# Linear attention and a mixture layer on one core: the denominators' signs summed in PSUM, their products moved to the end of the next pair's visit, and a new order

## The chip, the cores and the metric

The kernel runs on one core of a Trainium2 chip. The time is the device time of one execution in microseconds (us). Five queues work side by side on the core: TensorE (PE in the profile, PEld for its weight loads), VectorE (DVE), ScalarE (ACT), GpSimd (POOL) and SyncE (SP, which here only issues DMAs). Each of them takes its instructions strictly in the order in which the program has them, and an instruction that has to wait holds up all that stand behind it in its queue.

## The reference

There are 8 batches, 8 heads, 576 positions and a head dimension of 64. The features of queries and keys, `phi`, have 2 x 128 columns: the exponentials of both signs of a projection from which its largest absolute value has been taken. The output of the attention, with heads side by side, goes into a layer with 1024 hidden columns.

```
def phi(x):
    proj = einsum('bhsd,df->bhsf', x, w_phi)
    proj = proj - max(abs(proj), axis=-1, keepdims=True)
    return concatenate([exp(proj), exp(-proj)], axis=-1)
kv  = einsum('bhsf,bhsd->bhfd', phi(k), v)
z   = sum(phi(k), axis=2)
num = einsum('bhsf,bhfd->bhsd', phi(q), kv)
den = einsum('bhsf,bhf->bhs', phi(q), z) + 1e-06
x   = (num / den), heads joined: 4608 x 512
h   = x @ w_in
e   = exp(h - max(h));  solu = h * e / (sum(e) + 1e-09)
ln  = (solu - mean(solu)) / sqrt(var(solu) + 1e-06) * g_ln
out = ln @ w_out
```

So each position of each head has one denominator, a sum over 256 features, of which one half belongs to the sign + and one half to the sign -.

## The kernel before

**Tiling.** Two heads make a pair: there are 32 pairs. Two pairs make a unit `u`, of which there are 16, two for each batch; `sub` is the pair within the unit and `n = 2u + sub` its number. In a pair `j` is the head, `s` the sign and `c` the half of the 576 positions, 288 (`HC`) at a time. The second layer works on 36 tiles of 128 positions ("MoE" in names and comments). Nine of these tiles need the two batches of four units, and the last five of all need the last pair.

**What a pair does.** Keys are projected (`pjk`), reduced to their largest absolute value (`m`), subtracted (`dk`) and exponentiated (`ek`). A *visit* of TensorE (`visit`) then multiplies them with the values into the bank `kvT`, and at its end multiplies the summed exponentials `zacc` with ones (`kv_z`), so that `z` comes out 32 times over. VectorE turns the bank (`kvs`) and two steps of DMAs (`dk` in DRAM, then `kvf`) put it where it serves as weights. The queries are loaded by two DMAs of the same data, one for each half of the partitions (`rawq`), rounded (`hq`), corrected on GpSimd, projected (`pq`), turned (`blk`), given their maximum (`mtp`, `mt`, `mb`, `mcp`, `mcol`), turned back (`pT`) and exponentiated (`fq`).

**Numerators and denominators.** `q_num` multiplies `fq` with `kvf` into two banks `num`, one for each half of the positions. From pair 5 to pair 30 this stands at the *beginning* of the visit of the next pair (`JOIN = 6`); for the other six it is an operation of its own. `q_den` is always an operation of its own. It fills two banks `den`, one for each half of the positions; in each of them the rows 32 x (2s + j) and the 31 behind hold sign `s` of head `j`, 32 times the same row. ScalarE copies all four banks (`E`, `dE`). Then follows a chain over DRAM: `den_rows` stores each 32nd row of `dE` (`d<-dE`); `den_load` brings the 4 x 576 numbers back as 128 partitions x 2 signs x 9 (`cmp<-d`); VectorE adds the signs and the small constant and takes the reciprocal of 9 columns (`cmp`, `cmr`); `den_store` stores it (`d<-cmr`); `den_bcast` loads it in two DMAs to 64 partitions each (`rb<-d`). GpSimd multiplies `E` by `rb` (`divide`) into `xa` or `xb`, which the second layer reads.

**The second layer.** For each tile: `mxh` and `mxl` (two roundings of the input), `h` (24 matmuls in two halves), the maximum `nm`, the exponential `eu`, the product, the variance, the transpose `uT` in two parts, `uh` and `ul`, `o` (24 matmuls in two halves), `os` and the store of the output. These tiles are what TensorE does between the steps of the attention.

**What sets the order.** All operations are written down with an engine, a charged duration, their predecessors and the buffers that they take (`Plan.op`). `Plan.order` plays the program through, one operation at a time, with these durations. Where several operations are ready on an engine it takes the one with the smallest priority. The priority is the sum of two numbers from tables, `BASE` (the weights, the 16 units, the 36 tiles) and `OFFSET` (each kind of operation). A change of TensorE's tiled mode is charged (`SWITCH`) and avoided (`STICK`, `LINGER`). The result is one sequence, in which the instructions are emitted; on the chip each queue keeps its part of that sequence and waits by semaphores for what it needs. The charges and priorities have no other effect on the chip.

**Buffers.** There are three PSUM banks of the kind `a`. `pjk`, `pq`, `mtp`, `mcp`, `num` and `den` share them. There is one bank for `kvT`, and there are two tiles each for `E`, `dE` and `kvf` and one for `rb`.

The instructions go through a helper that keeps them in program order. For this reason nearly all rows of the profile name the same line, L347, and are told apart by the names of what they write and read.

Of the kernel before, what the change touches and what calls it, by code (L numbers as in the profile page):

```python
# [44 lines left out]
    rk=4, rv=5, xh=2, xl=2, m=3, d=3, e=6, za=2, kf=2, q4=5, m4=2, mt=2, mb=2, E=2, dE=2, rb=1,  # L45
# [22 lines left out]
)  # L68
OFFSET = (
# [49 lines left out]
)  # L119


# [1182 lines left out]
```

## Time and profile before

| | |
|---|---|
| median of 3 runs | 790.88 us (789.54 to 791.89) |
| the profiled execution, its own time | 790.95 us |
| its span, from the first to the last instruction | 789.2 us |
| granted TensorE clock, mean | 0.994 |
| DMAs issued for the denominators | 32 x (1 + 1 + 1 + 2) |

In a list of stretches, each row has the start and the end, the length, and for each engine its busy time and number of instructions, then the granted clock, the mean busy share of the DMA engines and the GB/s. In a timeline a row has its start, its length, the engine, the operation, what is written and what is read; in brackets stands the time that the engine had been idle, and what ended the idle time. Merged rows carry a count (x16). Rows of one matmul overlap, because matmuls are pipelined: what a matmul costs is read from start to start. In the chain of waits each row is a start, a length and a piece of work that the next one waited for. In a list of waits a row has who waited, for whom, the total in us, how often, and the longest. In a list of groups the last number before the bar is the mean of one instruction in ns, and behind the bar stands the idle time ahead of the group.

### The profile page before, as it was taken

The numbers are of one execution on the slowest core, as the hardware profiler recorded it, in microseconds if no ns is written. First come the engines' busy times: TensorE is split into PE (matmuls) and PEld (weight loads), VectorE is DVE, ScalarE is ACT, GpSimd is POOL, SyncE is SP. The second block draws the span as 40 slices with busy tenths as digits, with TensorE's granted clock in tenths as the row PEclk, the third lists the DMA queues.
The fourth block names the chain that finished last, engine by engine and source line by source line (L and its number), as shares of the span: only waits on it lengthen the run. The fifth ranks groups of instructions, "written<-read, shape, count | busy, mean of one in ns | idle before, by whom it ended". The sixth has DMA issues, their size and how long they took to land.

```text
span 789.2 us, 13661 instructions
## 1 busy us (share of the span) xinstructions
PE 756.7 (96%) x4935; PEld 562.2 (71%) x4935; DVE 486.4 (62%) x829; ACT 405.8 (51%) x814; POOL 470.9 (60%) x507
## 2 busy tenths in 40 slices
PE   5899898999999999999999999999999999999997
PEld 3565586767677777767776777777777776788886
DVE  4978684756675675756566686665756683444343
ACT  3876764564645565454745465463644655322322
POOL 1224897778687678585676759675776855231210
PEclk8999999999999999999999999999999999999999
DMA  6954442443526153442435343333334212200000
GB/s 203 374 122 122 104 103 52 108 110 104 119 73 135 53 123 104 106 100 70 125 81 121 85 108 100 90 88 92 87 99 114 78 43 78 52 28 14 27 28 27
DMA packets 105251, 75.96 MB, mean 96 GB/s; under 512 B 65376, under 2 KB 91488, under 8 KB 104672
## 3 DMA queue, kind: packets, MB, share of 16 engines
q1 hardware_dynamic: 105184, 75.10, 35.9%
q8 instruction: 39, 0.64, 0.4%
q14 instruction: 28, 0.23, 0.1%
HBM read 59.67 MB, written 15.38 MB: 95 GB/s over the span
## 4 chain that ended last, share of the span: by engine, by line
PE 72%; DMA 10%; DVE 5%; ACT 3%; POOL 3%; issue 3%; SPq 3%; ACTq 0%; POOLq 0%; DVEq 0%
PE o L347 21%; PE h L347 20%; PE kvT L347 9%; PE num L347 6%; PE pjk L347 5%; PE uT L347 3%; PE pq L347 3%; DMA rawq<-in_q 3%; PE den L347 3%; SPq L347 3%; DMA cmp<-d 2%; POOL hq L347 2%; DMA dk<-kvs 1%; PE pjq L347 1%; DMA rawk<-in_k 1%
## 5 line engine op out<-in xcount | busy, mean ns | idle before, releaser
L347 PE MATMUL o<-w_out_h,uh 128*128 128x512 f32 x288 | 116.0, 403 | 0.4 <-ACT uh L347 0.4
L347 ACT ACTIVATE ek<-dk 128x512 f32<-128x512 f32 (+1 forms) x160 | 87.2, 584 | 53.6 <-DVE dk L347 49.7
L347 PE MATMUL o<-w_out_h,ul 128*128 128x512 f32 x288 | 114.2, 397 | 0.0
L347 PE MATMUL o<-w_out_l,uh 128*128 128x512 f32 x288 | 113.9, 396 | 0.0
L347 POOL TENSOR_TENSOR zacc<-zacc,ek 128x512 f32<-128x512 f32 (+1 forms) x78 | 100.7, 1290 | 12.8 <-ACT ek L347 8.1
L347 POOL TENSOR_TENSOR hq<-rawq,hq 64x1152 fp32r<-64x1152 f32 x26 | 69.5, 2674 | 47.7 <-ACT hq L347 43.9
L347 PE MATMUL h<-win_h,mxh 128*128 128x512 f32 x288 | 93.6, 406 | 1.0 <-DVE eu L347 1.0
L347 PE MATMUL h<-win_h,mxl 128*128 128x512 f32 x288 | 90.8, 396 | 0.0
L347 PE MATMUL h<-win_l,mxh 128*128 128x512 f32 x288 | 90.6, 396 | 0.0
L347 DVE TENSOR_TENSOR ul<-uT,uh 128x512 fp32r<-128x512 f32 x72 | 48.2, 679 | 54.0 <-ACT uh L347 54.0
L347 ACT ACTIVATE fq<-pT 128x576 f32<-128x576 f32 x104 | 68.6, 688 | 17.3 <-DVE pT L347 14.0
L347 ACT CAST uh<-uT 128x512 fp32r<-128x512 f32 x72 | 41.6, 590 | 61.9 <-PE uT L347 48.8
L347 PE MATMUL num<-fq,kvf 128*64 128x288 f32 x512 | 69.2, 412 | 2.8 <-ACT win_h L347 1.8
L347 ACT ACTIVATE eu<-h,nm 128x1024 f32<-128x1024 f32 x36 | 40.3, 1118 | 57.6 <-DVE nm L347 57.5
L347 DVE TENSOR_REDUCE nm<-h 128x1 f32<-128x1024 f32 x36 | 43.8, 1218 | 41.7 <-PE h L347 41.6
L347 POOL TENSOR_TENSOR blk<-blk,mcol 128x1152 f32<-128x1152 f32 x26 | 55.6, 2137 | 17.2 <-ACT mcol L347 17.1
L347 PE MATMUL kvT<-ek,rawv 128*64 128x256 f32 x512 | 65.3, 387 | 0.0
L347 DVE STREAM_TRANSPOSE blk<-pq 128x288 f32<-128x288 f32 x104 | 46.5, 460 | 28.4 <-PE pq L347 22.8
L347 DVE TENSOR_TENSOR eu<-h,eu 128x1024 f32<-128x1024 f32 x36 | 43.9, 1220 | 32.4 <-ACT eu L347 32.4
L347 PEld LDWEIGHTS o<-w_out_h,ul 128*128 128x128 f32 x288 | 54.2, 188 | 13.6 <-DVE ul L347 0.4
L347 PEld LDWEIGHTS h<-win_h,mxl 128*128 128x128 f32 x288 | 54.2, 189 | 13.1 <-POOL mxl L347 0.2
L347 PEld LDWEIGHTS h<-win_l,mxh 128*128 128x128 f32 x288 | 54.1, 188 | 13.1
(107 smaller groups left out, 1584.1 us busy)
## 6 DMA issues: line engine op xcount, KB each, us to landing
rawq<-in_q SPq DMA_DIRECT2D x52, 288.0 KB
rb<-d SPq DMA_DIRECT2D x64, 144.0 KB
out<-os SPq DMA_DIRECT2D x36, 256.0 KB
rawk<-in_k SPq DMA_DIRECT2D x64, 128.0 KB
rawv<-in_v SPq DMA_DIRECT2D x64, 128.0 KB
dk<-kvs SPq DMA_DIRECT2D x28, 192.0 KB
kvf<-dk SPq DMA_DIRECT2D x112, 48.0 KB
wraw<-in_w_in SPq DMA_DIRECT2D x4, 1024.0 KB
```

The source lines that it names most:

```text
L347: return self.tc.keep_in_program_order(method(*args, **kwargs))
```

## The change

1. **Signs summed in PSUM.** `q_den` fills one bank instead of two. The rows 32 x (2c + j) now belong to half `c` of the positions and head `j`, and the matmul of the sign - is added to that of the sign +. The number and the shapes of the matmuls are as before: eight, each 32 columns of weights and 288 positions.
2. **The products' place.** For pairs 5 to 30 `q_den` stands at the end of the next pair's visit, behind `kv_z`. For the others it remains an operation of its own.
3. **One evacuation, and the reciprocal on VectorE at once.** ScalarE copies 128 x 288 once, and adds the small constant. VectorE inverts these 128 x 288 numbers in place.
4. **A shorter chain of DMAs.** `den_rows` stores each 32nd row of the inverted tile (4 x 288), and two DMAs broadcast it from there, each in two runs of 288 positions. `den_load` and `den_store` are gone. There are two `rb` tiles.
5. **One load of queries.** The input of the queries is laid out with its rows twice, and one DMA of 128 partitions replaces two of 64.
6. **New order.** Both tables are replaced, and several charged durations with them; the charge of the visit has the products in it, and the visit takes all three `a` banks in the plan. In the tables the entry of the weights goes from -200.2 to -223.1 and that of the first unit from -1092.1 to -1390.3.

```
-    ... E=2, dE=2, rb=1,
+    ... E=2, dE=2, rb=2,
...
 def visit(st, sub, before):
...
         kv_z(st, sub)
+    if before:
+        q_den(*before)
...
-def q_load(st, sub, i):
-    if i == 0:
-        st["rq", sub] = sb("q4", [P, 2, S], name="rawq")
-    nc.sync.dma_start(out=st["rq", sub][i * D : (i + 1) * D], in_=qT[st["b"], 2 * st["qd"] + sub])
+def q_load(st, sub):
+    st["rq", sub] = sb("q4", [P, 2, S], name="rawq")
+    nc.sync.dma_start(out=st["rq", sub], in_=qT[st["b"], 2 * st["qd"] + sub])
...
 def q_den(st, sub):
-    for c in range(2):
-        po = st["den", sub, c] = bank("a", [P, 512], "den")
-        for s in range(2):
+    po = st["den", sub] = bank("a", [P, 512], "den")
+    for s in range(2):
+        for c in range(2):
             for j in range(2):
-                r = slice(32 * (2 * s + j), 32 * (2 * s + j) + 32)
+                r, z = 32 * (2 * c + j), 32 * (2 * s + j)
                 nc.tensor.matmul(
-                    po[r, :HC], lhsT=st["kvf", sub][:, 2, r], rhs=st["qf", sub, c][:, j, s],
-                    start=True, stop=True,
+                    po[r : r + 32, :HC], lhsT=st["kvf", sub][:, 2, z : z + 32], rhs=st["qf", sub, c][:, j, s],
+                    start=(s == 0), stop=(s == 1), skip_group_check=True,
                 )
...
+def den_eps(st, sub):
+    st["dens", sub] = sb("dE", [P, HC], name="dE")
+    nc.scalar.activation(out=st["dens", sub], in_=st["den", sub][:, :HC], func=AF.Copy, bias=EPS)
+
+def den_recip(st, sub):
+    nc.vector.reciprocal(out=st["dens", sub], in_=st["dens", sub])
+
 def den_rows(st, sub):
-    st["d1", sub] = dram.tile([4, S], F32, tag="d1", name="d1")
+    st["d1", sub] = dram.tile([4, HC], F32, tag="d1", name="d1")
     nc.sync.dma_start(out=st["d1", sub], in_=st["dens", sub][::32, :])
-
-def den_load(st, sub):
-    st["cmp", sub] = work.tile([P, 2, 9], F32, tag="cmp", bufs=8, name="cmp")
-    nc.sync.dma_start(out=st["cmp", sub], in_=st["d1", sub].rearrange("(s h) (a b) -> (h a) s b", s=2, b=9))
-
-def den_recip(st, sub):
-    c = st["cmp", sub]
-    nc.vector.scalar_tensor_tensor(
-        out=c[:, 0], in0=c[:, 0], scalar=EPS, in1=c[:, 1], op0=ALU.add, op1=ALU.add
-    )
-    st["cmr", sub] = work.tile([P, 9], F32, tag="cmr", bufs=8, name="cmr")
-    nc.vector.reciprocal(out=st["cmr", sub], in_=c[:, 0])
-
-def den_store(st, sub):
-    st["d2", sub] = dram.tile([2, S], F32, tag="d2", name="d2")
-    nc.sync.dma_start(out=st["d2", sub].rearrange("h (a b) -> (h a) b", b=9), in_=st["cmr", sub])
 
 def den_bcast(st, sub, j):
     if j == 0:
         st["rb", sub] = sb("rb", [P, S])
+    src = st["d1", sub].rearrange("(c j) t -> j c t", j=2)[j : j + 1]
     nc.sync.dma_start(
-        out=st["rb", sub][j * D : (j + 1) * D, :], in_=st["d2", sub][j : j + 1, :].to_broadcast([D, S])
+        out=st["rb", sub][j * D : (j + 1) * D, :].rearrange("p (c t) -> p c t", c=2),
+        in_=src.to_broadcast([D, 2, HC]),
     )
...
-add(("qd", sub), "tensor", 2 * mm32(HC), z + 5.5, q_den, (sub,), feat + [source["num"]],
-    [("a", ("den", sub, c)) for c in range(2)], fk, {(u, "qv", sub, 0, "den"): mm32(HC)})
+if not joined:
+    add(("qd", sub), "tensor", 2 * mm32(HC), z + 5.5, q_den, (sub,), feat + [source["num"]],
+        [("a", ("den", sub))], fk)
...
+add(("dc", sub), "vector", dve(HC) + 30, z + 6.3, den_recip, (sub,), [("de", sub)], (), [("dE", sub)])
...
-BASE = (-200.2, -1092.1, ...)
+BASE = (-223.1, -1390.3, ...)
-OFFSET = (...)
+OFFSET = (...)
```

More of the change, by code (lines that the diff above doesn't have):

```diff
@@ L142, in dma @@
 def dma(nbytes, spread=False):
[L143 removed]
+    return (580 if spread else 400), max(nbytes / 360.0, 50)
 class Plan:
@@ L542, in linear_attention_then_moe @@
         op(("wl", i), "sync", dma(8 * P * DF), z - 9, w_load, (i, raw_tag[i] if i < 4 else None), alloc=[(raw_tag[i], R)] if i < 4 else [])
-        op(("ws", i), "scalar", 947, z, w_rebias, (i,), [("wl", i)], tiles=R4)
+        op(("ws", i), "scalar", 1055, z, w_rebias, (i,), [("wl", i)], tiles=R4)
         op(("wb", i, 0), "vector", 600, z, w_bits, (i, 0, w_tag[i]), [("ws", i)], [(w_tag[i], T)], R4)
@@ L550, in linear_attention_then_moe @@
         else:
-            op(("wg", i), "scalar", 1226, z, w_gain, (i,), [("wb", i, 2), "gain"], tiles=[T])
+            op(("wg", i), "scalar", 1260, z, w_gain, (i,), [("wb", i, 2), "gain"], tiles=[T])
     for i in range(5, 8):
@@ L884, in q_den, with q_oe @@
                     )
-    def q_oe(st, sub, c, key):
+    def q_oe(st, sub, c):
         if c == 0:
-            st[key + "s", sub] = sb("E" if key == "num" else "dE", [P, S], name="E" if key == "num" else "dE")
-        nc.scalar.copy(out=st[key + "s", sub][:, c * HC : (c + 1) * HC], in_=st[key, sub, c][:, :HC])
+            st["nums", sub] = sb("E", [P, S], name="E")
+        nc.scalar.copy(out=st["nums", sub][:, c * HC : (c + 1) * HC], in_=st["num", sub, c][:, :HC])
+    def den_eps(st, sub):
+        st["dens", sub] = sb("dE", [P, HC], name="dE")
+        nc.scalar.activation(out=st["dens", sub], in_=st["den", sub][:, :HC], func=AF.Copy, bias=EPS)
@@ L1008, in linear_attention_then_moe @@
                 tiles += [("abs", (pu, "f", ps_, c)) for c in range(2)] + [("abs", (pu, "kf", ps_))]
-                alloc += [("a", ("abs", (pu, "num", ps_, c))) for c in range(2)]
-                early = {(pu, "qv", ps_, c, "num"): cost + (1 - c) * 2 * mm32(HC) for c in range(2)}
-                cost += 4 * mm32(HC)
+                alloc += [("a", ("abs", (pu, "num", ps_, c))) for c in range(2)] + [("a", ("abs", (pu, "den", ps_)))]
+                den = 2 * mm32(HC)
+                early = {(pu, "qv", ps_, c): den + cost + (1 - c) * 2 * mm32(HC) for c in range(2)}
+                early[u, "kve", sub] = den
+                cost += 4 * mm32(HC) + den
             add(("V", sub), "tensor", cost, z, visit, (sub, (states[pu], ps_) if joined else None), after, alloc, tiles,
@@ L1041, in linear_attention_then_moe @@
             if qsp:
-                for i in range(2):
-                    add(("ql", sub, i), "sync", dma(D * 2 * S * 4, True), z - 4, q_load, (sub, i),
-                        [("ql", sub, 0)] if i else (), () if i else [("q4", ("rq", sub))], [("rq", sub)])
-                add(("qh", sub), "scalar", act(2 * S), z - 2.5, q_hi, (sub,), [("ql", sub, 1)], [("q4", ("hq", sub))],
+                add(("ql", sub), "sync", (400, 1640), z - 4, q_load, (sub,), (), [("q4", ("rq", sub))])
+                add(("qh", sub), "scalar", act(2 * S), z - 2.5, q_hi, (sub,), [("ql", sub)], [("q4", ("hq", sub))],
                     [("rq", sub)])
-                add(("qlo", sub), "gpsimd", pool(2 * S), z - 2.2, q_lo, (sub,), [("qh", sub)], (),
+                add(("qlo", sub), "gpsimd", pool(2 * S) + 130, z - 2.2, q_lo, (sub,), [("qh", sub)], (),
                     [("rq", sub), ("hq", sub)])
@@ L1094, in linear_attention_then_moe @@
             joined = JOIN <= n + 1 < 4 * B
-            source = {"num": ("abs", ((n + 1) // 2, "V", (n + 1) % 2)) if joined else ("qo", sub), "den": ("qd", sub)}
+            visitor = ("abs", ((n + 1) // 2, "V", (n + 1) % 2))
+            source = {"num": visitor if joined else ("qo", sub), "den": visitor if joined else ("qd", sub)}
             if not joined:
@@ L1102, in linear_attention_then_moe @@
             for c in range(2):
-                for k, t in (("num", "E"), ("den", "dE")):
-                    add(("qv", sub, c, k), "scalar", act(HC, True), z + 5.1 + c, q_oe, (sub, c, k),
-                        [source[k]] + ([("qv", sub, 0, k)] if c else []),
-                        () if c else [(t, (t, sub))], [(k, sub, c), (t, sub)])
-            add(("dr", sub), "sync", dma(16 * S), z + 6.4, den_rows, (sub,),
-                [("qv", sub, 0, "den"), ("qv", sub, 1, "den")], (), [("dE", sub)])
@@ L1109, in linear_attention_then_moe @@
-            add(("dl", sub), "sync", dma(0), z + 6.8, den_load, (sub,), [("dr", sub)], ())
-            add(("dc", sub), "vector", 330, z + 7.3, den_recip, (sub,), [("dl", sub)])
-            add(("ds", sub), "sync", dma(0), z + 7.4, den_store, (sub,), [("dc", sub)])
+                add(("qv", sub, c), "scalar", act(HC, True), z + 5.1 + c, q_oe, (sub, c),
+                    [source["num"]] + ([("qv", sub, 0)] if c else []), () if c else [("E", ("E", sub))],
+                    [("num", sub, c), ("E", sub)])
@@ L1112, in linear_attention_then_moe @@
+            add(("de", sub), "scalar", act(HC, True), z + 6.0, den_eps, (sub,), [source["den"]], [("dE", ("dE", sub))],
+                [("den", sub)])
+            add(("dc", sub), "vector", dve(HC) + 30, z + 6.3, den_recip, (sub,), [("de", sub)], (), [("dE", sub)])
+            add(("ds", sub), "sync", (330, 100), z + 6.5, den_rows, (sub,), [("dc", sub)], (), [("dE", sub)])
             for j in range(2):
[L1113 to L1114 removed]
+                add(("db", sub, j), "sync", (560, 600), z + 6.9, den_bcast, (sub, j),
+                    [("ds", sub)] + ([("db", sub, 0)] if j else [("db", 0, 1)] if sub else []), () if j else [("rb", ("rb", sub))],
@@ L1115, in linear_attention_then_moe @@
                     [("rb", sub)])
             pair = 2 * qd + sub
-            after = [(u, "db", sub, 1), (u, "qv", sub, 1, "num")] + ([(2 * b, "dv", 0)] if pair else [])
+            after = [(u, "db", sub, 1), (u, "qv", sub, 1)] + ([(2 * b, "dv", 0)] if pair else [])
             op((u, "dv", sub), "gpsimd", pool(S) + (130 if b % 2 else 30), z0 + (z + 8.5) * step, divide,
@@ L1219, in linear_attention_then_moe @@
     op("tail", "gpsimd", 0, 2 * B * UNIT + 40, start_tail, (),
-       [(2 * B - 1, "qv", s, c, k) for s in range(2) for c in range(2) for k in ("num", "den")])
+       [(2 * B - 1, "qv", s, 1) for s in range(2)] + [(2 * B - 1, "de", s) for s in range(2)])
     for t in range(NTOK // P):
@@ L1253, in linear_attention_then_moe @@
             op(n("o", hf), "tensor", 12 * mm(512), z + 13 + 3 * hf, moe_o, (t, hf),
-               [n("ul", hf)] + ([n("o", 0)] if hf else [("wol", f) for f in range(8)] if t == 0 else []),
+               [n("ul", hf)] + ([n("o", 0)] if hf else [("wol", f) for f in range(8)]),
                () if hf else [("mo", n("o"))], [n("uh"), n("ul"), n("o")])
```

22 lines of the change are left out of this document (10 added, 12 removed), and 104 rows, old and new, of tables (BASE, OFFSET).

## The prediction

> **What bounds the kernel now.** I read the page first (busy shares), then the stretches, then the rows of TensorE that follow an idle time, then the chain of waits ahead of those rows. The page:
>
> ```profile
> span 789.2 us, 13661 instructions
> PE 756.7 (96%) x4935; PEld 562.2 (71%) x4935; DVE 486.4 (62%) x829; ACT 405.8 (51%) x814; POOL 470.9 (60%) x507
> ```
>
> TensorE is the bound: it stands idle for 789.2 - 756.7 = 32.5 us in all. The stretches show where:
>
> ```profile
> core 0: us, PE busy (x) PEld busy (x) DVE busy (x) ACT busy (x) POOL busy (x), PEclk, DMA share, GB/s
> 0.00:20.00 20.00, 11.09 (x29) 7.97 (x31) 8.33 (x16) 6.27 (x12) 2.26 (x17) 0.86 0.68 206
> 20.00:40.00 20.00, 17.34 (x141) 11.09 (x143) 18.04 (x24) 17.96 (x33) 4.74 (x2) 0.93 0.99 369
> 340.00:380.00 40.00, 38.26 (x232) 29.63 (x226) 25.20 (x45) 19.67 (x42) 25.06 (x30) 1.00 0.37 95
> ...
> 700.00:740.00 40.00, 40.00 (x185) 32.51 (x184) 16.77 (x22) 9.91 (x17) 7.24 (x15) 1.00 0.06 21
> ```
>
> The first 40 us hold 11.57 us of the idle time, with the DMA engines nearly full in the second half of it. In the middle it comes in pieces (1.74 us in the 40 us from 340). The end (700 to 740) is TensorE without a gap. So a cheaper instruction on another engine gives nothing by itself. Time comes from fewer cycles on TensorE or from an idle time that goes away. The idle times that this change can reach are these:
>
> ```profile
> 36.87 0.55 PE L347 MATMUL dT<-ident,dq 128*128 128x128 f32 x3 [1.61 <-ACT dE L347]
> 70.47 1.13 PE L347 MATMUL pjq<-wph,rawq 128*128 128x256 f32 x4 [0.47 <-DVE dk L347]
> 172.17 0.38 PE L347 MATMUL pjk<-wph_h,xh 128*128 128x256 f32 x1 [1.64 <-ACT dE L347]
> 208.90 0.40 PE L347 MATMUL pq<-hq,w_hh 128*128 128x288 f32 x1 [0.54 <-POOL hq L347]
> 350.62 0.38 PE L347 MATMUL pq<-hq,w_hh 128*128 128x288 f32 x1 [1.33 <-DVE dk L347]
> 432.12 0.69 PE L347 MATMUL den<-fq,kvf 128*32 128x288 f32 x8 [0.51 <-ACT E L347]
> 584.98 0.29 PE L347 MATMUL mtp<-ident,m 128*36 128x128 f32 x1 [1.42 <-DVE m L347]
> ```
>
> Three of them look like VectorE's ordinary work, but the chain of waits ahead of 350.62, and likewise of 432.12, shows what held VectorE:
>
> ```profile
> 347.20 1.89 DMA cmp<-d
> 349.11 0.57 DVE cmp L347
> 349.84 0.64 DVE dk L347
> ...
> 420.90 5.10 DMA cmp<-d
> 426.02 1.57 DVE cmp L347
> 427.83 1.09 DVE nm L347
> ```
>
> VectorE's queue is in order. It stands at the denominators' addition until a DMA has landed, and all that is behind it is late: the keys' subtraction dk at 349.84, the row maximum nm at 427.83. Ahead of 70.47 and 584.98 the chain has the same links.
>
> **The change, part by part.** *The products move (A).* Eight matmuls (16 instructions) before, eight of the same shape after; what can change is the entry to and the exit from the column-tiled mode. The timeline has both places already:
>
> ```profile
> 449.55 0.42 PE L347 MATMUL kvT<-zacc,ones 128*32 128x128 f32 x8
> 449.91 0.41 PE L347 MATMUL pq<-hq,w_hh 128*128 128x288 f32 x1
> ...
> 463.73 0.40 PE L347 MATMUL o<-w_out_l,uh 128*128 128x512 f32 x1
> 463.96 0.39 PE L347 MATMUL o<-w_out_h,ul 128*128 128x512 f32 x1
> 464.29 1.18 PE L347 MATMUL den<-fq,kvf 128*32 128x288 f32 x16
> 465.39 0.40 PE L347 MATMUL pq<-hq,w_hh 128*128 128x288 f32 x1
> ...
> 474.32 0.42 PE L347 MATMUL kvT<-zacc,ones 128*32 128x128 f32 x8
> 474.56 1.15 PE L347 MATMUL den<-fq,kvf 128*32 128x288 f32 x16
> 475.64 0.29 PE L347 MATMUL mtp<-ident,m 128*36 128x128 f32 x1
> ```
>
> Start to start, a visit's end alone takes 449.91 - 449.55 = 0.36 us. A lone set of products takes 1.10 (464.29 to 465.39) and the matmul before it 0.33 (463.96 to 464.29), where its neighbour takes 0.23 (463.73 to 463.96): 1.20 in all. Both together, as the change has them, take 475.64 - 474.32 = 1.32. The move saves 0.36 + 1.20 - 1.32 = 0.24 us. It applies to pairs 5 to 30, 26 of them; in 11 of these the products already follow the visit in the trace (474.56 is one). So A = 15 x 0.24 = -3.6 us; its bounds are 0 (if an exit costs the same wherever it stands and the new order opens as many) and -3.6.
>
> *VectorE's wait goes (B).* Per pair the change takes off VectorE an addition, a reciprocal of 9 columns and the wait ahead of them, and puts a reciprocal of 288 columns there, which waits only for ScalarE:
>
> ```profile
> L347 DVE SCALAR_TENSOR_TENSOR cmp<-cmp 128x9 f32<-128x9 f32 x32 | 18.1, 567 | 40.7 <-DMA cmp<-d 40.7
> L347 DVE RECIPROCAL cmr<-cmp 128x9 f32<-128x9 f32 x32 | 6.9, 216 | 1.1
> L347 DVE BATCH_NORM_AGGREGATE mv<-bst 128x2 f32<-128x12 f32 x36 | 7.5, 209 | 1.8
> L347 DVE TENSOR_TENSOR dk<-pjk,m 128x512 f32<-128x512 f32 x64 | 43.0, 672 | 0.8
> L347 DVE TENSOR_TENSOR dk<-pjk,m 128x256 f32<-128x256 f32 x16 | 6.5, 408 | 0.0
> ```
>
> Before, that is 40.7 / 32 + 0.567 + 0.216 = 2.05 us of VectorE per pair. The wide reciprocal is not in the trace. The two dk rows give (672 - 408) / 256 = 1.03 ns per column and 144 ns fixed; at that rate 288 columns take 0.44 us, the low bound. If all of the small reciprocal beyond 144 ns goes by column, a column costs (216 - 144) / 9 = 8 ns, and 288 of them 2.45 us, the high bound. I take 0.44: the aggregate, which takes 12 columns in and two out, costs 209 ns too, so 216 looks like the floor of a short instruction rather than nine slow columns. Then VectorE has 1.6 us more per pair, and the idle times at 70.47, 350.62, 432.12 and 584.98 lose their cause: B = -(0.47 + 1.33 + 0.51 + 1.42) = -3.7 us. What would be late next shows in none of these chains, since dk and nm start as soon as VectorE is free, so I count it whole; bounds 0 and -3.7.
>
> The Trainium skill, "VectorE: DVE Perf Modes", section "First, the fixed hardware budget", says that the reciprocal is an iterated divide with a repeat count of 8. Read as eight cycles a column, an estimate from its 0.96 GHz is 288 x 8 / 0.96 = 2.4 us, against the change; the small reciprocal's row fits that reading as well as mine. What that would do to the time is the first rival.
>
> *One bank instead of two (C).* Two evacuations by ScalarE become one, and one of the three "a" banks is held instead of two. The waits at 36.87 and 172.17 are for such an evacuation, 1.61 + 1.64 = 3.25 us. The first evacuation stays, and what it queues behind on ScalarE stays too, so I take half: C = -1.6 us, bounds 0 and -3.25. The 12.5 us of ScalarE that go (half of 25.3) are worth nothing more:
>
> ```profile
> L347 ACT COPY dE<-den 128x288 f32<-128x288 f32 x64 | 25.3, 401 | 13.1 <-PE den L347 12.2
> ```
>
> *The queue of SP (D).* Two of five DMAs per pair go (the load into cmp, the store of cmr); the chain d, cmp, d, rb becomes d, rb. The broadcast reads two runs of 288 values instead of one of 576, in as many bytes. The two loads of rawq become one of 128 partitions.
>
> ```profile
> 197.80 0.54 SPq L347 DMA_DIRECT2D cmp<-d  x1
> 198.39 0.48 SPq L347 DMA_DIRECT2D rawq<-in_q  x1
> ```
>
> ```profile
> SPq L347 <- DVE cmr L347: 58.8, 23, 5.3
> SPq L347 <- DMA d<-cmr: 28.1, 27, 2.1
> ```
>
> SP is in order too, and loads of k, v and q queue behind these waits. Here the second half of a rawq is issued behind a cmp, 0.59 us after it. What that load feeds reaches TensorE late at 208.90 (0.54 us). D = -0.5 us; bounds 0 and -2.1, that row and the 1.64 us at 172.17 together, whose chain also goes back to a rawq. What SP now waits for, the reciprocal, comes before the landing that it waited for. A second rb tile lets a broadcast start before the previous pair's multiplication has read its own; that multiplication is on GpSimd, off the path while MoE tiles fill TensorE.
>
> *The new order.* Priorities and several charged costs are replaced; the charges time nothing on the chip, they only order the queues. I can't read the resulting order from the tables and put it at 0. It can close part of the other idle time: 32.5, less the 11.57 of the first 40 us and the 5.8 of B, C and D, is 15.1 us. A third of that, -5.0, is as much as I allow it. And it can open waits; that is the third rival.
>
> **Sum.** -3.6 - 3.7 - 1.6 - 0.5 = -9.4. The profiled execution took 790.95 us (1.75 around its span), and the median of the runs is 790.88, so it stands for them: 790.95 - 9.4 = 781.5 us. Nothing is earned or lost behind pair 31: its products stay apart, and the shorter chain ends where TensorE has MoE tiles without a gap (700 to 740).
>
> **Rivals.** *The wide reciprocal is slow.* At 2.45 us it holds VectorE longer than the old steps did (2.05 per pair), at the same places. B then is not -3.7 but +3.7 x (2.45 / 2.05 - 1) = +0.7, and 790.95 - 3.6 + 0.7 - 1.6 - 0.5 = 786.0 us. For it: 72 ns over nine columns; against it: the aggregate's 209 ns.
>
> *The visit needs all three "a" banks.* The two banks of the numerators and one of the denominators are written in one visit, and the small transposes or projections right behind it want an "a" bank at once (mtp at 475.64). If ScalarE copies late, each of the 26 visits is followed by a wait of the length of one copy, 0.40 us: 26 x 0.40 = +10.4, and the time is 790.95 - 9.4 + 10.4 = 792.0 us, no change. For it: the wait of 0.51 at 432.12 is of this kind. Against it:
>
> ```profile
> 473.18 0.40 ACT L347 COPY E<-num 128x288 f32<-128x288 f32 x1
> ```
>
> This copy is the second of the visit, so both numerator banks are free at 473.58, 2.06 us before mtp starts, so only an overloaded ScalarE decides for it, and it gets lighter.
>
> *The front loads in another order* (the other side). In the first 40 us the DMA engines are the limit (0.99 at 369 GB/s). One weight load of 1024 KB ahead of keys and queries that were ahead of it costs 1.049 MB / 369 GB/s = 2.8 us of TensorE. With four of the eight moved ahead the gain is gone (+11.4), with five the time is 790.95 - 9.4 + 14.2 = 795.8 us. For it: most of the idle time lies there already, and all priorities change. Against it: the base of the first unit falls by 298, that of the weights only by 23.
>
> **How the numbers follow.** The forecast, 781.5, has 0.56: the parts are in the code whatever the order. Its own range is 775 (order -5.0 and C at its bound, 781.5 - 6.65) to 787 (B and C at 0, 781.5 + 5.3). The slow reciprocal, 786.0, has 0.14. The banks, 792.0, have 0.17, and the front, 795.8, has 0.10; 0.03 is left for a time below the range, where the order closes more than I allow. About 0.3% (2.4 us) is what a measurement of this kernel can tell from no change. Below 788.5 lie the forecast, the rest and most of the slow reciprocal, and a third of the banks: 0.56 + 0.03 + 0.12 + 0.05 = 0.76. Above 793.3 lie the front and a little of the banks: 0.11. Between: 0.13. The range for 8 in 10 is 775 to 791.5.
>
> **What would show it.** A: rows of kvT<-zacc are followed by den in 26 visits, and TensorE's idle time falls by less than the time does. B: the reciprocal's mean is near 0.44 us and VectorE waits for no DMA of denominators. C: no wait of TensorE is put down to dE. D: no cmp and no cmr among the DMA issues, and SP's waits for them gone. If the reciprocal's row says 2.4, or TensorE waits for E or dE behind the visits, or the first 40 us hold over 20 us of idle time, the forecast is wrong in that step.

## The result, and the profile after

The changed kernel takes 799.38 us (median; 798.39 to 803.94) where the kernel before took 791.38 in the same comparison: a ratio of 1.0125, with a 95% interval of 1.0096 to 1.0153. It is 8.0 us slower; the forecast was 9.4 us faster.

The page of the kernel after (span; busy time by engine; the chain that ended last; the group of the new reciprocal):

```profile
span 796.6 us, 13504 instructions
...
PE 755.1 (95%) x4935; PEld 564.8 (71%) x4935; DVE 521.2 (65%) x797; ACT 395.6 (50%) x782; POOL 470.7 (59%) x507
...
PE 68%; DVE 12%; DMA 6%; POOL 5%; SPq 3%; issue 3%; ACT 3%; POOLq 0%; DVEq 0%; ACTq 0%
...
L345 DVE RECIPROCAL dE<-dE 128x288 f32<-128x288 f32 x32 | 62.3, 1947 | 32.4 <-ACT dE L345 32.4
```

VectorE, which was to be relieved, is busy for 521.2 us instead of 486.4, and has 12% of the chain (5% before). The one new instruction takes 1947 ns, 62.3 us in 32 pairs. The forecast had 440 ns for it. Ahead of it VectorE waits for ScalarE's evacuation, 32.4 us in all; the forecast put this wait at nothing. Before, it waited 40.7 us for the DMA into `cmp`.

The stretches of the kernel after, those of the prediction and two longer ones (start, end, length; busy time of PE, PEld, DVE, ACT, POOL; clock, DMA share, GB/s):

```profile
0.00:20.00 20.00, 8.88 (x20) 5.59 (x20) 6.01 (x12) 6.00 (x10) 2.25 (x17) 0.89 0.71 230
20.00:40.00 20.00, 17.22 (x132) 11.07 (x134) 19.97 (x25) 15.89 (x28) 2.37 (x1) 0.85 0.75 283
340.00:380.00 40.00, 38.73 (x264) 28.69 (x263) 28.38 (x50) 22.28 (x45) 31.96 (x35) 1.00 0.37 111
700.00:740.00 40.00, 40.00 (x186) 32.48 (x185) 17.91 (x24) 11.96 (x22) 10.44 (x20) 1.00 0.08 28
...
40.00:200.00 160.00, 148.18 (x1166) 106.18 (x1159) 118.95 (x173) 91.09 (x197) 107.41 (x94) 1.00 0.37 105
200.00:700.00 500.00, 488.69 (x3203) 367.82 (x3202) 337.88 (x539) 256.67 (x505) 341.51 (x360) 1.00 0.32 91
```

The same two longer stretches of the kernel before:

```profile
40.00:200.00 160.00, 150.94 (x1182) 108.71 (x1183) 112.75 (x189) 97.62 (x210) 112.19 (x99) 0.99 0.43 105
200.00:700.00 500.00, 492.34 (x3201) 366.19 (x3198) 310.74 (x554) 260.38 (x522) 337.40 (x357) 1.00 0.36 91
```

TensorE's idle time (length less PE busy) was 11.6 us to 40 us, 9.1 from there to 200 and 7.7 from there to 700. It is now 13.9, 11.8 and 11.3: 8.7 us more in these three, spread over all of them. The end is without a gap as before. VectorE's busy time in the middle stretch has grown by 27.1 us.

What the reciprocal does there stands in the chain of waits of the kernel after, ahead of an idle time of TensorE (start, length, piece of work):

```profile
215.74 1.01 PE den L345 x16
216.75 0.02 issue
216.77 0.42 ACT dE L345
217.19 0.02 issue
217.22 1.95 DVE dE L345
219.17 0.15 DVE mt L345
219.32 0.04 issue
219.36 0.54 PE pq L345 x2
```

The timeline of TensorE at the same place, and at a visit with its products:

```profile
218.08 0.29 PE L345 MATMUL pq<-hq,w_l 128*128 128x288 f32 x1
219.36 0.40 PE L345 MATMUL pq<-hq,w_hh 128*128 128x288 f32 x1 [0.99 <-DVE mt L345]
...
491.61 0.43 PE L345 MATMUL kvT<-zacc,ones 128*32 128x128 f32 x8
491.85 1.15 PE L345 MATMUL den<-fq,kvf 128*32 128x288 f32 x16
492.94 0.66 PE L345 MATMUL uT<-ident,eu 128*128 128x128 f32 x4
```

The wait for a DMA on VectorE has gone, and a longer instruction stands in its place: the queries' maximum `mt` is queued behind 1.95 us of division, and `pq`, which needs the bank that `mt` reads, comes 0.99 us late. The rows from 491.61 show that the move itself did what was said: start to start, the visit's end and the products take 1.33 us (the prediction had 1.32).

The list of waits of the kernel after (who for whom: us in total, times, longest) has these rows for the new steps; SP's waits for `cmr` and VectorE's for `cmp` are gone from it:

```profile
ACT dE L345 <- PE den L345: 52.5, 24, 3.1
DVE dE L345 <- ACT dE L345: 32.4, 25, 4.5
...
PE dT L345 <- ACT dE L345: 0.3, 1, 0.3
```

and SP's own list:

```profile
SPq L345 <- DVE dE L345: 24.5, 6, 10.8
```

So SP waits for the inverted tile in six pairs instead of for `cmr` in 23 (58.8 us), and of TensorE's matmuls only one waits for the evacuation, for 0.3 us (two of its weight loads do, 0.8 us together).

### The profile page after: what moved, and what is told of

It is laid out like the page before. It is cut to its first block, busy times and chain, and to the rows that moved or that the text cites. A ratio compares the mean times of both kernels' runs of the same rounds, so it can differ in the third digit from the quotient of the medians.

```text
span 796.6 us, 13504 instructions
## 1 busy us (share of the span) xinstructions
PE 755.1 (95%) x4935; PEld 564.8 (71%) x4935; DVE 521.2 (65%) x797; ACT 395.6 (50%) x782; POOL 470.7 (59%) x507
## 4 chain that ended last, share of the span: by engine, by line
PE 68%; DVE 12%; DMA 6%; POOL 5%; SPq 3%; issue 3%; ACT 3%; POOLq 0%; DVEq 0%; ACTq 0%
PE h L345 20%; PE o L345 19%; PE kvT L345 7%; PE num L345 7%; PE pjk L345 4%; DVE dE L345 4%; PE uT L345 3%; PE den L345 3%; SPq L345 3%; DVE w L345 2%; PE pq L345 2%; DMA rawq<-in_q 2%; DVE m L345 2%; POOL zacc L345 1%; DMA rb<-d 1%
## 5 line engine op out<-in xcount | busy, mean ns | idle before, releaser
L345 ACT ACTIVATE ek<-dk 128x512 f32<-128x512 f32 (+1 forms) x160 | 88.9, 583 | 52.9 <-DVE dk L345 46.6
L345 DVE RECIPROCAL dE<-dE 128x288 f32<-128x288 f32 x32 | 62.3, 1947 | 32.4 <-ACT dE L345 32.4
L345 PE MATMUL num<-fq,kvf 128*64 128x288 f32 x512 | 70.8, 419 | 4.7 <-DMA kvf<-dk 4.7
L345 PEld LDWEIGHTS o<-w_out_h,uh 128*128 128x128 f32 x288 | 54.2, 188 | 12.5 <-DVE ul L345 1.2
L345 PEld LDWEIGHTS o<-w_out_l,uh 128*128 128x128 f32 x288 | 54.3, 189 | 11.3
```

The source lines that it names most:

```text
L345: return self.tc.keep_in_program_order(method(*args, **kwargs))
```

## The experiments

All ratios are against the kernel before, timed in the same comparison, with 95% intervals. The first nine change the kernel after, or put its one suspect into the kernel before.

### The reciprocal cut to 9 columns

```
-nc.vector.reciprocal(out=st["dens", sub], in_=st["dens", sub])
+nc.vector.reciprocal(out=st["dens", sub][:, :9], in_=st["dens", sub][:, :9])
```

> The changed kernel in its own order, with VectorE's reciprocal over 9 of the 288 columns; the denominators are set to 1 and the numerators scaled by a constant, so the division is left out. Two theories. Slow reciprocal: its 1.95 us (1947 ns in the row) is what the change lost; with 0.22 us in its place the forecast's sum comes true, 780 to 787 us. New order: the queues' new sequence opens waits of its own; then 1.7 us less on VectorE changes little, 794 to 799 us.

Measured: 782.84 us, ratio 0.9916 (0.9884 to 0.9949). Its page and its groups (mean ns of one behind the bar, then the idle time of the engine ahead of the group):

```profile
span 779.7 us, 13504 instructions
...
PE 748.3 (96%) x4935; PEld 564.5 (72%) x4935; DVE 472.5 (61%) x797; ACT 396.4 (51%) x782; POOL 470.3 (60%) x507
...
L345 DVE RECIPROCAL dE<-dE 128x9 f32<-128x9 f32 x32 | 6.7, 210 | 34.5 <-ACT dE L345 34.5
...
L345 PE MATMUL pq<-hq,w_hh 128*128 128x288 f32 x104 | 32.1, 318 | 0.3 <-ACT fq L345 0.3
```

The last of these groups in the kernel after:

```profile
L345 PE MATMUL pq<-hq,w_hh 128*128 128x288 f32 x104 | 32.8, 324 | 6.5 <-DVE blk L345 2.7 <-ACT mcol L345 1.7 <-DVE mt L345 1.0
```

All of the change but the length of one instruction gains 7 us. The length costs 16.5 us (799.38 - 782.84), the whole loss and more. Ahead of the queries' projections alone the idle time goes from 0.3 to 6.5 us.

Both kernels have the same 4935 matmuls in the same order, so the start of each can be set against its start in the other trace. Of the 16.9 us between the two spans, 8.1 arise at these projections (`pq<-hq,w_hh`), most of them in pieces of about 1 us, and 3.6 at the numerators. Only a part of the 16.9 us is idle time of TensorE: that is 41.5 us instead of 31.4, and the busy time is 755.1 us instead of 748.3. One source of the longer busy time shows in the trace of the kernel after: behind an idle time of 2.38 us (the numerators at 298.54, waiting for `kvf`) the granted clock is 0.57 from 299 to 303 us, and 1.00 in the three us that follow. What makes up the rest of it is open.

### Half of the columns

```
+nc.vector.reciprocal(out=st["dens", sub][:, :144], in_=st["dens", sub][:, :144])
```

> As the run with the reciprocal of 9 columns (782.8 us), with 144 columns: 160 + 6.2 x 135 = some 1.0 us of VectorE instead of 0.22. Loss in proportion to the hold: half of the way to 799, 789 to 793 us. Loss only from the point where the hold outruns the slack that the order left: 782 to 787 us, and nearly all of the loss lies between 1.0 and 1.95 us.

Measured: 786.16 us, ratio 0.9962 (0.9939 to 0.9985). Its group:

```profile
L345 DVE RECIPROCAL dE<-dE 128x144 f32<-128x144 f32 x32 | 33.5, 1047 | 34.6 <-ACT dE L345 34.6
```

The first 0.84 us of length (210 to 1047 ns) cost 3.3 us of time, the next 0.90 us (to 1947) cost 13.2 (3.6 and 12.9 by the ratios; the intervals of the two short ones overlap, that of 288 columns lies apart). TensorE's idle time is 31.4, 34.6 and 41.5 us at the three lengths. A loss in proportion to the length would have put this run near 791.

### A second reciprocal of 288 columns

```
+nc.vector.reciprocal(out=spare, in_=spare)
```

ahead of the first one, in the kernel after.

> The changed kernel with a second reciprocal of 128x288, on a spare tile, ahead of each of the 32: VectorE gets 32 x 1.95 = 62 us more. Slow reciprocal: the loss goes by the length of the hold, so at least as much again as from 0.22 to 1.95 us: 808 to 825 us. New order: VectorE is busy 65% of the span and has room, 799 to 805 us.

Measured: 831.3 us, ratio 1.0519 (1.0479 to 1.0559). Another 61.4 us on VectorE cost 31.9 us, about half of their length.

### The same instruction in the kernel before

A reciprocal of 288 columns of a spare tile, behind each of the 32 short ones; nothing else changed.

> The kernel before with a reciprocal of 128x288 on a spare tile behind each of its 32 short ones: VectorE gets 62 us more, nothing else changes, and the order is the old one, made without it. Slow reciprocal: slower by 8 to 20 us, 799 to 811 us. New order: VectorE has room in the old order, 791 to 795 us.

Measured: 828.07 us, ratio 1.0482 (1.044 to 1.0524). Its group:

```profile
L347 DVE RECIPROCAL spare<-spare 128x288 f32<-128x288 f32 x32 | 60.6, 1894 | 0.0
```

The length is that of the instruction, not of the changed kernel: 1894 ns. It costs 38 us where nothing is taken away for it, against the 16.5 us above. This suggests that the rest of the change gave VectorE room and that the instruction used it up; no run separates this from the new order.

### The true price charged in the order

```
-add(("dc", sub), "vector", dve(HC) + 30, ...
+add(("dc", sub), "vector", 1880, ...
```

> The changed kernel with one charge of the plan altered: the reciprocal is charged 1880 ns instead of 398, so the order is made for what it takes. Slow reciprocal, and only because the order didn't know it: most of the loss comes back, 786 to 792 us. Slow reciprocal whatever the order: 795 to 801 us. New order: no direction, 793 to 805 us.

Measured: 833.3 us, ratio 1.0546 (1.0506 to 1.0586): not better but 34 us worse. To tell the order from the instruction, that order was run with the short reciprocal:

> The order made with the reciprocal charged at 1880 ns (833 us with the real one), now with the reciprocal of 9 columns; the division is left out as there. If that order was bad by itself, because the priorities were fitted to other charges: far above the 782.8 us of the same instructions in the changed kernel's order, 805 to 825 us. If it is good and the long reciprocal was the whole of its loss: 780 to 795 us.

Measured: 831.28 us, ratio 1.0512 (1.0478 to 1.0545). The length of the instruction hardly matters there, so the order itself is bad. One charge altered alone gives another order, presumably because the priorities were fitted to the charges that they stand beside, and this pair says nothing on whether an order made for 1.9 us could hide them.

### Another engine for the division

ScalarE takes the logarithm at the evacuation and then exp(-ln); VectorE has no reciprocal.

```
-nc.scalar.activation(out=st["dens", sub], in_=st["den", sub][:, :HC], func=AF.Copy, bias=EPS)
+nc.scalar.activation(out=st["dens", sub], in_=st["den", sub][:, :HC], func=AF.Ln, bias=eps_col)
...
-nc.vector.reciprocal(out=st["dens", sub], in_=st["dens", sub])
+nc.scalar.activation(out=st["dens", sub], in_=st["dens", sub], func=AF.Exp, scale=-1.0)
```

> The changed kernel with the same sequence, in which ScalarE inverts: its evacuation takes the logarithm (with the small constant) and a second activation of 128x288 the exponential of its negative; VectorE has no reciprocal at all. All of the computation is in it. Slow reciprocal: VectorE loses 62 us of work, ScalarE gets 32 x 0.4 = 13 us; as with the reciprocal of 9 columns, 780 to 787 us. Any order made for another length: ScalarE, too, now takes time that the order did not know, 788 to 796 us. If the logarithm needs another table of functions, 64 loads of some 1.3 us come on top, over 800 us.

Measured: 822.56 us, ratio 1.0423 (1.0405 to 1.044). A group that had one member has 65:

```profile
L345 ACT ACT_TABLE_LOAD x65 | 83.4, 1283 | 7.9 <-DMA wph<-in_w_phi 6.7
```

Each change between logarithm and exponential loads a table, 1283 ns. One load of a set that has both functions, at the start, takes them away:

```
+nc.scalar.add_instruction(mybir.InstLoadActFuncSet(..., act_func_set_id=6, ...))
```

> The earlier run in which ScalarE inverts by exp(-ln), with one table that holds both functions loaded at the start instead of 65 loads of 1.28 us. All of the computation is in it; VectorE has no reciprocal, ScalarE has 32 activations of 0.4 us more than the changed kernel. If the reciprocal on VectorE alone is what the change lost: 780 to 787 us, faster than both kernels. If any work that the order doesn't know costs as much: 788 to 794 us.

Measured: 783.86 us, ratio 0.9926 (0.9904 to 0.9949). The groups:

```profile
L345 ACT ACTIVATE dE<-den,eps_col 128x288 f32<-128x288 f32 x32 | 16.0, 500 | 55.3 <-PE den L345 55.3
L345 ACT ACTIVATE dE<-dE 128x288 f32<-128x288 f32 x32 | 14.1, 440 | 0.4
L389 ACT ACT_TABLE_LOAD x1 | 1.3, 1283 | 0.7 <-PEq L1292 0.7
```

With 0.94 us of ScalarE, of which 0.42 was there already, in place of 1.95 of VectorE, the change is 6 us faster than the kernel before instead of 8 slower. All of the computation is done here, so the short reciprocal's 782.84 was no effect of the data that it left out.

### The products back out of the visit

The kernel with 9 columns, its products put one operation of TensorE behind the visit instead of at its end:

> As the run with the reciprocal of 9 columns, but the denominators' products stand one operation of TensorE behind the visit instead of at its end (26 pairs). Term A as the prediction priced it: 26 x 0.24 us = 6.2 us more than that run, 787 to 790.5 us. The move saves nothing, because an exit from the tiled mode costs the same wherever it stands: within 1.5 us of that run, 781 to 784.5 us.

Measured: 790.44 us, ratio 1.0019 (0.9999 to 1.0038), 7.6 us more than with the products in the visit by the medians, 8.1 by the ratios. The price of an entry and an exit for 26 pairs was 26 x 0.24 = 6.2 us. The loss is TensorE's work and not waiting: its busy time is 757.7 us against 748.3, its idle time 31.8 against 31.4.

The next runs change the kernel *before*, one part at a time, in its own order.

### VectorE's wait taken away

The addition and the reciprocal of 9 columns read a tile of constants; the five DMAs stay.

> The kernel before, in which VectorE's addition and reciprocal read a constant tile instead of the landed denominators, so VectorE no longer waits for that DMA; all DMAs stay, the inverted sums are left out. Term B as the prediction priced it, -3.7 us: 785 to 789 us. Rival: what comes next on VectorE is late anyway, within 1.5 us of the kernel before.

Measured: 785.5 us, ratio 0.9953 (0.9935 to 0.9972): -3.3 us by the medians, -3.7 by the ratio. The matmuls are those of the kernel before, in the same order. Three of the four that stood idle in the prediction's term B, for 1.33, 0.51 and 1.42 us, start in this trace without a gap. The fourth stands idle for longer, 1.07 us instead of 0.47.

### One load of queries

```
-nc.sync.dma_start(out=st["rq", sub][i * D : (i + 1) * D], in_=qT[...])
+    nc.sync.dma_start(out=st["rq", sub], in_=qT[...])
```

> The kernel before in its own sequence, with the two loads of rawq joined to one of 128 partitions (the second of the two operations issues nothing). Term D as the prediction priced it: -0.5 us, no more than -2.1, so 788 to 791 us, no difference that shows. Rival: a DMA of 576 KB lands later than the first half of two, and ScalarE's rounding of the queries with it: 791 to 795 us.

Measured: 784.64 us, ratio 0.9932 (0.9911 to 0.9954), -5.2 us. In the kernel before TensorE had three idle times between 160 and 212 us, at 172.17 (1.64), 205.29 (0.96) and 208.90 (0.54). Here that stretch of TensorE's timeline has one:

```profile
202.67 0.74 PE L347 MATMUL h<-win_h,mxh 128*128 128x512 f32 x2 [2.58 <-DVE eu L347]
```

This matmul starts 2.62 us earlier than in the kernel before (205.29), though the idle time in the stretch is only 0.56 us shorter (3.14 before). The gain is thus only in part one of the idle times that were named. Matmul by matmul, the lead over the trace of the kernel before grows most at its matmuls of 129.10 (2.2 us; `uT`, which had been idle for 2.05), 172.17 (1.6), 584.98 (1.4) and 350.62 (1.1), and 2.5 us of it are lost again at 402.32. The idle times at 584.98 and 350.62 are two of those that term B counted for VectorE's wait, and VectorE's wait for `cmp` is 24.2 us in this kernel instead of 40.7. So B and D reach in part for the same idle times.

### One bank and one evacuation

The signs summed in one bank, ScalarE copying once; the chain keeps its five DMAs (the first two with half of the numbers), and the wait and the two loads are as before.

> The kernel before in its own sequence, with the signs summed in one bank and one evacuation by ScalarE; the five DMAs, VectorE's addition (now of zeros) and reciprocal of 9 columns and the two loads of rawq stay. All of the computation is in it. Term C as the prediction priced it, -1.6 us with the bounds 0 and -3.25: 786.5 to 791 us. What the run with all parts leaves for it beside B (-3.7) and D (-5.3) is about -2.7 us. Rival: ScalarE's lighter load helps beyond the bank: below 786.5 us.

Measured: 794.46 us, ratio 1.0057 (1.004 to 1.0075): 4.4 us *slower*. A row of the kernel before's list of waits:

```profile
ACT dE L347 <- PE den L347: 12.2, 11, 4.5
```

and rows of this kernel's list:

```profile
ACT dE L347 <- PE den L347: 20.0, 18, 5.0
...
PEld pq L347 <- ACT dE L347: 2.0, 7, 0.3
...
PE pjk L347 <- ACT dE L347: 2.0, 3, 1.7
...
PE dT L347 <- ACT dE L347: 1.7, 1, 1.7
```

The one copy stands in ScalarE's queue where half of the products used to be copied, so ScalarE waits there for all eight (20.0 us instead of 12.2), and what takes that bank next waits for the copy; seven waits of `pq` (of its weight loads) are new. Matmul by matmul, about 2 us of the 4.3 by which this trace falls behind arise at these seven `pq`, some 0.3 us each; the rest is gains and losses at many places. The two idle times on which the prediction's term C rested (1.61 us at `dT`, 1.64 at `pjk`) have not gone with the second evacuation: 1.7 us each. Does the loss pass through VectorE's wait for the chain over DRAM, which starts later too? That was asked by taking this wait away as well:

> The kernel before with the signs summed in one bank and one evacuation (the edit that alone measured +4.5 us), and now with VectorE's addition and reciprocal reading a tile of constants, so that VectorE waits for no landing of denominators; the five DMAs of the chain stay. Left out: the division by the true denominators (the reciprocals are 1, the numerators are scaled). Theory 1: the one bank loses because the copy starts only behind all eight products, so the chain over DRAM starts and lands later and VectorE and what is queued behind its wait is late; without the wait the loss goes, and the time is that of the same kernel with two banks and no wait, 785.5 us, or up to 2 us under it. Theory 2: the loss sits in TensorE's products or in ScalarE's queue and doesn't pass through VectorE's wait; then the time is 785.5 + 4.5 = 790 us.

Measured: 788.87 us, ratio 1.0007 (0.9989 to 1.0025). With the wait, one bank adds 0.0057; without it 0.0054 (1.0007 - 0.9953). So most of the loss doesn't pass through the wait. Then the place was changed:

```
 if key == "den":
     if c == 0:
         st["dens", sub] = sb("dE", [P, HC], name="dE")
+    else:
         nc.scalar.copy(out=st["dens", sub], in_=st["den", sub][:, :HC])
```

and the products use the second of the two banks that the old order keeps for them.

> As the kernel before with the signs summed in one bank and one evacuation (which measured +4.5 us), but the products use the bank that the old order gives to the second half of the positions, and ScalarE's one copy stands at the place of the second half's copy instead of the first's. All of the computation is done. Theory 1: the +4.5 us are the place: the copy of all eight products stood where four had been copied, so ScalarE's queue stood longer (its wait in front of dE is 23.2 us against 13.3 with two banks, both without VectorE's wait) and that bank came free later. Then this kernel loses nothing against the kernel before: ratio 0.997 to 1.001, 788.5 to 791.5 us. Theory 2: the loss has another cause, and the ratio stays at 1.0057, 795 us.

Measured: 791.69 us, ratio 1.003 (1.0015 to 1.0046). About half of the loss goes and 2.0 us stay (2.4 by the ratio): between the two theories, with an interval that overlaps that of the 794.46 us. By this run the place of the copy and the bank is likely one cause; what the rest is isn't settled.

### The parts together in the old order

First the bank, the evacuation, the shorter chain and exp(-ln) with the joint table, still with two loads of queries:

> The kernel before with the signs summed in one bank, one evacuation, the reciprocal as exp(-ln) on ScalarE and the shorter chain of DMAs; the input of the queries is still loaded by two DMAs. All of the computation is done. If the gains of the parts add up, joining the loads is worth 5.3 us here too, and the time is 778.25 + 5.3 = 783.6 us. If the shorter chain had taken away the same waits on SP as the joined load does, the time is near 778 us, and if the joined load carried most of the gain of 11.7 us, it is near 788 us.

Measured: 785.47 us, ratio 0.9952 (0.9936 to 0.9968). Then with one load:

> The kernel before in its own sequence, with the signs summed in one bank, one load of rawq, the shorter DMA chain and ScalarE's exp(-ln) behind its evacuation, but the products where they were and the old order. All of the computation is in it. By the prediction's terms without A: -3.7 - 1.6 - 0.5 = -5.8, 783 to 788 us. If the gain needs the new order or the move: 788 to 793 us.

Measured: 778.25 us, ratio 0.9852 (0.9825 to 0.9878). The joined load is worth 7.2 us here (7.9 by the ratios). The shorter chain is worth the difference of 785.47 and 794.46, 9.0 us (8.3 by the ratios): VectorE has no wait and no division, and SP issues three DMAs instead of five. The same kernel with VectorE's reciprocal of 288 columns in place of ScalarE's:

> As the run of 778.3 us with the parts of the change in the old sequence, but the inversion is the change's own: ScalarE copies once, VectorE takes the reciprocal of 128x288, directly behind the evacuation. If the reciprocal's hold alone makes the loss, whatever the order: 16 us (799.4 - 782.8) on top, 792 to 797 us, and the new order would be no better than the old one. If the old order has less room for it, as with the dummy reciprocals (+38 us): 805 to 818 us, and the new order had made up for part of it.

Measured: 796.98 us, ratio 1.0091 (1.0066 to 1.0115): +18.7 us. The instruction makes the loss in the old order as in the new one.

Last, the two moves of the copy and the bank in the kernel of 778.25 us:

> The best version so far (old order, signs in one bank, one load of queries, shorter chain, exp(-ln) on ScalarE; 778.25 us) with the same two moves: the bank and ScalarE's place of the second half of the positions. All of the computation is done. If the place costs 4.5 us here too, 774 us; if the shorter chain has left no one to wait for that bank or behind that copy, 778 us as before.

Measured: 773.48 us (773.07 to 773.9), ratio 0.9793 (0.978 to 0.9807), the fastest of all. Rows of the list of waits, first of the kernel of 778.25 us:

```profile
ACT dE L347 <- PE den L347: 27.7, 25, 5.0
...
PEld pq L347 <- ACT dE L347: 2.8, 7, 0.4
PEld pjk L347 <- ACT dE L347: 1.6, 8, 0.2
PEld dT L347 <- ACT dE L347: 1.6, 2, 1.2
```

then of the kernel of 773.48 us, in whose list TensorE waits for `dE` nowhere:

```profile
ACT dE L347 <- PE den L347: 19.2, 15, 5.1
```

Matmul by matmul, this kernel gains 3.1 us at `pq`, in seven places, and 1.6 at `pjk`, of 4.05 in all. One of the seven, first in the kernel of 778.25 us, then here:

```profile
452.87 0.29 PE L347 MATMUL pq<-hq,w_l 128*128 128x288 f32 x1
453.32 0.40 PE L347 MATMUL pq<-hq,w_hh 128*128 128x288 f32 x1 [0.16 <-ACT dE L347]
...
451.14 0.30 PE L347 MATMUL pq<-hq,w_l 128*128 128x288 f32 x1
451.28 0.29 PE L347 MATMUL pq<-hq,w_hh 128*128 128x288 f32 x1
```

From start to start this step takes 0.45 us behind the copy of the products and 0.14 where the copy and the bank have moved.

Its page and its stretches:

```profile
span 771.7 us, 13428 instructions
...
PE 751.0 (97%) x4935; PEld 563.2 (73%) x4935; DVE 468.1 (61%) x765; ACT 412.6 (53%) x814; POOL 471.3 (61%) x508
...
40.00:200.00 160.00, 157.27 (x1240) 114.97 (x1241) 115.74 (x181) 106.83 (x224) 118.72 (x106) 1.00 0.39 114
200.00:700.00 500.00, 498.71 (x3224) 375.53 (x3223) 298.29 (x508) 262.89 (x517) 334.64 (x359) 1.00 0.31 88
```

Between 40 and 700 us TensorE stands idle for 4.0 us, against 16.7 in the kernel before and 23.1 in the kernel after. Of the 20.7 us of idle time that are left in the span, 12.0 lie in the first 40 us.

## Why the prediction was wrong

**The step that failed: the price of the wide reciprocal.** It had bounds of 0.44 and 2.45 us, and I took 0.44, because 209 ns of another short instruction made 216 ns look like a floor. Measured are 210 ns for 9 columns, 1047 for 144 and 1947 for 288. That is a straight line: (1047 - 210) / 135 = 6.2 ns a column and (1947 - 210) / 279 = 6.2. So 56 of the 210 ns were the nine columns after all. Both readings fitted the one row; the choice between bounds 2 us apart, times 32, was made by likeness with an instruction of another kind. The Trainium skill, "VectorE: DVE Perf Modes", section "First, the fixed hardware budget", has the reciprocal as an iterated divide; the estimate of 2.4 us from its repeat count of 8 was 0.5 too high, and a good deal nearer than my 0.44.

**The rival had the mechanism, but not the size.** "The wide reciprocal is slow" said that VectorE would be held longer at the same places, and gave 786.0 us. The price that it set on this was wrong in two ways. First, it left out a wait that the whole prediction put at nothing: VectorE stands ahead of the reciprocal until ScalarE has copied, 32.4 us in 25 of the 32 pairs. Second, it was in proportion to the mean time that VectorE is held. With the division alone, 1.95 us (under the 2.05 before), this rule would have given a small gain; with the wait, 32.4 / 32 + 1.95 = 2.96 us, it gives +3.7 x (2.96 / 2.05 - 1) = +1.6 and 786.9 us, still far from 799.38. The 2.05 before were for the larger part a wait (40.7 us in 32 pairs), and taking that wait away earned only 3.7 us; the run with 9 columns has the new wait too (34.5 us) and takes 782.84 us; but the 55.6 us of division (62.3 - 6.7) cost 16.5. A wait and an instruction of the same mean length are not worth the same here. The row of the wait in the kernel before's list is

```profile
DVE cmp L347 <- DMA cmp<-d: 40.7, 19, 5.5
```

Its total lay in 19 of the 32 pairs, and by the small gain most of it where nobody behind it was late, while the division stands in all 32, ahead of the queries' maximum and the keys. And the loss isn't linear: 3.3 us for the first 0.84 us, 13.2 for the next 0.90. I read this as room that VectorE has, which the first part takes up.

**Without that step the number would have come out, in part by chance.** The change with nine columns takes 782.84 us, with exp(-ln) 783.86; forecast were 781.5. The terms behind it did not all hold: the runs put A and D higher than the sum had them, and C and the order lower:

- **A, the products (-3.6).** Right in mechanism: undone, they cost 7.6 us, where the price of 0.24 us for 26 pairs gives 6.2. The sum counted only the 15 pairs whose products stood alone in the old order; at 7.6 / 26 they are worth 4.4 us. The trace after shows the products behind `kvT<-zacc` in 26 visits as was said, the trace before in 11.
- **B, VectorE's wait (-3.7).** Right in size and for the most part in mechanism: -3.3 to -3.7 with the wait alone taken away, and three of its four idle times are gone there. The fourth, at 70.47, grew, so a part of the gain came from elsewhere. Nor were the four tied to this one cause alone: the joined load shortens or removes three of them too.
- **C, one bank (-1.6, bounds 0 and -3.25).** Wrong in sign in the old order: +4.4 us, outside the bounds. The evacuation that went was counted as a gain, and the two idle times behind the sum stayed (1.7 us each); the one at 172.17 goes with the joined load, so it was D's. That the evacuation that stays must wait for all eight products, at the place of the first four, was not seen. With the copy and its bank at the later place the loss is 2.0 us alone, and 4.8 us are gained in the kernel with all the parts. In the changed kernel itself the order is another and hardly any wait for `dE` is left (0.3 us in the row above), so what C is worth there is not known.
- **D, SP's queue (-0.5, bounds 0 and -2.1).** Too small, outside its bounds: the joined load alone is worth 5.2 us, 7.2 beside the shorter chain. I had counted the one idle time at which a row named `hq`, with the one at 172.17 as the far bound. The half load reached further: the lead of that run arises at `uT`, `pjk`, `mtp` and `pq` as well.
- **The new order (0).** It costs. The kernel with exp(-ln) and the new order takes 783.86 us, that with the old order and the products where they were 778.25, which is 5.6 us less although the move of the products (3.6 to 4.4 us for 15 pairs) is missing there. So the new order loses 9 to 10 us, and 14 to 15 against 773.48. This is an estimate from runs of two comparisons, and it counts with the order the second `rb` tile and the banks that the plan reserves for the visit. The order wasn't readable from the tables, as was said, but zero was not the neutral value for it. That the old order had been fitted to the parts that stayed is a guess. The charge of the reciprocal (398 ns for 1947) is not the whole of it, as the two runs with the true charge show; what in the tables causes it is open.

**The other rivals.** *The banks*: no; one matmul waits for `dE`, 0.3 us, and none for `E`, and that one is not behind a visit. *The front*: no; the first 40 us hold 13.9 us of idle time, 2.3 more than before and far from the 20 named.

**The signs that were named** did their work: the first row to look at was the reciprocal's mean, and "if the reciprocal's row says 2.4 ... the forecast is wrong in that step" was answered by 1.95.

## What to carry to other kernels

An instruction that the trace doesn't show is a bound and not a price, and when both bounds fit the one short row there is, the time at the far bound deserves a chance near that of the forecast; a row of the same operation at another width would have settled it. A hold on an in-order engine need not be worth the wait of the same mean length that it replaces: ask what is queued behind it at each place, and be ready for a loss that rises faster than the length, as it did here. An idle time that one part of a change removes may go with another part too, so terms read from idle times need not add up. Merging two steps also merges their waiting: try the merged step where the later one stood.

## What the runs showed of the hardware that was not expected

- VectorE's reciprocal of fp32 takes about 6.2 ns a column of 128 partitions and some 154 ns beside (210 - 9 x 6.2), where the subtraction `dk` takes 1.03 ns a column. ScalarE's exp(-ln) of the same tile takes 500 + 440 ns.
- Logarithm and exponential in turn cost a table load of 1283 ns at each change, 65 of them and 39 us of the kernel's time (822.56 against 783.86); one load of a set that holds both, ahead of all else, removes them.
- Two loads of the same 288 KB for two halves of the partitions against one of 576 KB in a queue that is otherwise the same: 5.2 and 7.2 us of 790. In the place that the prediction showed, the second half was issued only 0.59 us behind a load of `cmp`.
